# Gate and up weights side by side on two queues, and a new written order around the handover to the gate/up stage

## The chip, the core and the metric

The kernel runs on one core of one Trainium2 chip. A core has five engines that run their own instruction streams and meet through semaphores: TensorE (PE; its weight loads are listed as PEld), VectorE (DVE), ScalarE (ACT), GpSimd (POOL) and SyncE (SP). Transfers are started from SP or ACT and run on sixteen DMA engines. The metric is the time of one execution on the device, in microseconds (us); lower is better.

## What is computed

A pre-LayerNorm block on 2048 tokens of width 448 in bf16: a linear attention with 16 heads of 28, and a gated feed-forward of width 1792, each with a residual.

```python
def _A_ref(x, wqkv, wo):
    q, k, v = qkv[0], qkv[1], qkv[2]              # x @ wqkv, 16 heads of 28
    phi = lambda t: jnp.where(t > 0, t + 1, jnp.exp(t)) + 1e-6
    pq, pk = phi(q), phi(k)
    kv = jnp.einsum("bhsd,bhse->bhde", pk, v)     # sums over all tokens
    z = jnp.einsum("bhsd->bhd", pk)
    num = jnp.einsum("bhqd,bhde->bhqe", pq, kv)
    den = jnp.einsum("bhqd,bhd->bhq", pq, z)[..., None] + 1e-6
    o = num / den
    return o.reshape(B, S, D) @ wo
def _B_ref(x, w_gate, w_up, w_down):
    h = _gelu(x @ w_gate) * (x @ w_up)
    return h @ w_down
h = x + _A_ref(_layernorm(x), A_wqkv, A_wo)
h2 = h + _B_ref(_layernorm(h), B_w_gate, B_w_up, B_w_down)
```

The sum over all tokens parts the kernel in two: no token's attention output exists before the last token's k and v.

## The kernel before

The 2048 tokens are 16 tiles of 128. All work is cut into named tasks, each on one engine; a task waits by semaphores for the tasks whose data it reads or whose buffers it overwrites. In which order an engine runs its tasks is written out by hand in five strings, `ORDERS`, one for each of PE, ACT, DVE, POOL and SP; an engine goes through its string strictly in turn. The names, with the tile's number behind them:

- Start: `warm0`, `warm1` are matmuls of ones that only keep PE busy; POOL writes `ones`, `ident` and the zero columns of `o_sb` (`opad`, `opad2`). DVE takes the statistics (`bnst`, `bnag`), ACT `ln` and `rstd`, DVE or POOL the normalized tile (`norm`). Tiles 0 to 3 are transposed on PE (`tr`, evacuated by ACT's `ev`), tiles 4 to 15 by DMA transposes on SP (`xT`).
- k and v: `k`, `v` (PE), then phi(k): `ek` (ACT), `cl` (a clamp, POOL), `ph` (DVE), and `evv` (ACT) for v; `acc` adds to the kv sums in banks 6 and 7; DVE's `kz1`, `kz2` mask them.
- q: eight tasks for four chunks of 512 tokens, each in two halves, `qa` and `qb`; phi(q) by `eq`, `rq` (ACT), `cq`, `pq`.
- Attention output: `nd` (PE), `rd`, `om` (DVE: reciprocal, product), then o transposed. For tiles 0 and 1 PE does it (`tro`, evacuated by ACT's `evo`), for the others DMA transposes on SP (`oT`). `wo` (PE) and `hr` (DVE, the residual) follow; then the second LayerNorm (`hbnst`, `hbnag`, `hln` and `hrstd` on ACT, or `vpe`, `pow` on POOL; `normh`), `wrap` (DVE copies columns again behind the row) and the transposed tile: PE's `trh` with `evh` for tiles 0 and 1, SP's `hT` for the others.
- Gate and up: `gu0` to `gu55`, in chunks of 2, 2, 4, 4 and 4 tiles; ACT's `ge` (gelu, two per task) and DVE's `hm` (the product, two per task). Then `down`, `out` (DVE) and `dout` (SP).

Most matmuls use half of the array: a pair works on rows 0 to 63 and 64 to 127 at once. A product then comes in two tasks (k and v, qa and qb, `nd2a` and `nd2b`, `wo4a` and `wo4b`), the second with the row groups exchanged between two PSUM banks, and so it waits for the first. `tro`, `trh`, `wo0` and `wo1` use all 128 rows.

The gate and up weights lie in one tile `wgu_sb`, gate in partitions 0 to 63, up in 64 to 127. SP loads them in fourteen pieces, gate and up in turn, behind the last `xT` and the four `wo` loads and ahead of `oT2`, `oT3` and the load of the down weights (`dwd`). A gate/up task of the first two chunks computes two blocks of 128 columns for 256 tokens in 28 matmuls; a task of the later chunks one block for 512 tokens in 14.

Of the kernel before, what the change touches and what calls it, by code (L numbers as in the profile page):

```python
# [912 lines left out]
```

## Time and profile before

| | us |
|---|---|
| runs shown: median (lowest to highest of 3) | 196.68 (196.2 to 196.69) |
| the profiled execution | 196.7 |
| its span, first to last instruction | 194.9 |
| PE busy | 190.3 |
| DVE busy | 116.3 |
| ACT busy | 78.2 |
| POOL busy | 42.0 |
| granted TensorE clock, mean | 0.999 |

The span is what the trace covers; the rest of an execution's time lies around it. A row of the timeline begins with start and duration in us, then engine, line, operation, the tile written and those read, the shapes, how many instructions it stands for, and in brackets how long the engine was idle before it and what ended that. Rows overlap where instructions are pipelined, so that the distance of two starts tells more than a duration. In the chain of work the program is followed back from its last instruction; each row is a stretch with the engine and line that held it. All matmuls that come in pairs have one line, that of a helper (L430), and are told apart by their tiles.

### The profile page before, as it was taken

How to read it: one execution, taken by the hardware profiler on the slowest of the kernel's cores; microseconds unless marked ns; L12 is line 12 of the kernel's file. 1: busy time of each engine (PE TensorE's matmuls, PEld its weight loads, DVE VectorE, ACT ScalarE, POOL GpSimd, SP SyncE). 2: the span in 40 equal slices, each digit the busy share in tenths (PEclk: the TensorE clock that was granted, in tenths of full speed). 3: DMA queues.
4: the chain of work that ended last, by engine and by line, in shares of the span. 5: the costliest groups of instructions: out<-in, count | busy, mean ns of one | idle time of the engine just before them, and what ended most of it. 6: DMA issues, size and time to landing. Idle time of an engine off the chain costs nothing.

```text
span 194.9 us, 5336 instructions
## 1 busy us (share of the span) xinstructions
PE 190.3 (98%) x2192; PEld 137.9 (71%) x2192; DVE 116.3 (60%) x301; ACT 78.2 (40%) x205; POOL 42.0 (22%) x90
## 2 busy tenths in 40 slices
PE   7999999999999999999999999999999999999994
PEld 7556658754588977976675577877778779899554
DVE  2989735368998946843967745756735443431512
ACT  3689866669784212220442441233232442411100
POOL 3099974300050310500500500500500000000000
PEclk9999999999999999999999999999999999999999
DMA  6944558999836052152062250172040000010111
GB/s 191 377 116 97 81 110 185 247 248 205 260 103 110 15 101 50 50 105 62 10 129 46 46 106 2 30 117 51 5 94 28 23 0 0 3 47 3 47 47 47
DMA packets 37256, 17.53 MB, mean 90 GB/s; under 512 B 28272, under 2 KB 36336, under 8 KB 37232
## 3 DMA queue, kind: packets, MB, share of 16 engines
q1 hardware_dynamic: 36352, 16.45, 36.8%
q10 hardware_dynamic: 880, 0.75, 1.2%
q8 instruction: 17, 0.28, 0.6%
q14 instruction: 7, 0.06, 0.1%
HBM read 8.72 MB, written 1.84 MB: 54 GB/s over the span
## 4 chain that ended last, share of the span: by engine, by line
PE 96%; issue 1%; ACT 1%; DVE 1%; POOL 0%; DVEq 0%; ACTq 0%; POOLq 0%
PE ps L430 87%; PE ps L780 6%; PE ps L454 2%; DVE x_sb L660 1%; PE ps L495 1%; ACT xn L617 1%; PE ps L681 0%; ACT xnT L523 0%; PE ps L672 0%; DVE x_sb L756 0%; POOL ones_bf L395 0%; POOL eps_t L398 0%; ACT pqT L616 0%; DVEq L196 0%; ACTq L196 0%
## 5 line engine op out<-in xcount | busy, mean ns | idle before, releaser
L430 PE MATMUL ps<-hnT,wgu_sb 64*128 64x512 bf16 (+1 forms) x980 | 90.4, 333 | 0.0
L430 PEld LDWEIGHTS ps<-hnT,wgu_sb 64*128 64x128 bf16 x980 | 64.5, 94 | 18.6 <-DVE hh L832 1.7
L830 ACT ACTIVATE gl<-ps 128x256 bf16<-128x256 f32 x112 | 36.9, 381 | 89.3 <-PE ps L430 88.2
L832 DVE TENSOR_TENSOR hh<-ps,gl 128x256 bf16<-128x256 f32 x112 | 42.5, 415 | 35.7 <-ACT gl L830 31.5
L430 PE MATMUL ps<-wd_sb,hh 64*128 64x448 bf16 x336 | 34.4, 349 | 0.0
L430 PEld LDWEIGHTS ps<-wd_sb,hh 64*128 64x128 bf16 x336 | 25.6, 94 | 6.2 <-DVE x_sb L756 0.2
L430 PE MATMUL ps<-wkv_sb,xnT 64*128 64x448 bf16 x192 | 22.4, 350 | 0.4 <-ACT xnT L523 0.4
L462 DVE BATCH_NORM_STATS2 st<-x_sb 128x6 f32<-128x448 bf16 x32 | 18.7, 611 | 2.6 <-DMA x_sb<-in_A_x_dram 2.6
L756 DVE TENSOR_TENSOR x_sb<-ps,x_sb 128x448 bf16<-128x448 f32 (+1 forms) x17 | 9.9, 591 | 16.6 <-PE ps L430 9.8
L474 POOL TENSOR_SCALAR ln<-mv 128x2 f32<-128x2 f32 x7 | 1.6, 223 | 75.0 <-DVE mv L463 74.9
L568 DVE SCALAR_TENSOR_TENSOR pk<-ps,tm 128x448 bf16<-128x448 f32 x16 | 9.8, 620 | 9.6 <-POOL tm L566 7.1
L430 PE MATMUL ps<-xnT,wq_sb 64*128 64x512 bf16 x112 | 14.9, 377 | 0.2 <-ACT xn L617 0.2
L430 PEld LDWEIGHTS ps<-wkv_sb,xnT 64*128 64x128 bf16 x192 | 10.1, 94 | 6.3 <-issue 0.8
L430 PE MATMUL ps<-wo_sb,oT 64*128 64x448 bf16 x98 | 12.1, 350 | 0.1
L660 DVE TENSOR_TENSOR x_sb<-ps,x_sb 128x448 bf16<-128x448 f32 x16 | 9.4, 618 | 4.6 <-PE ps L430 4.4
L780 PE MATMUL ps<-wd_sb,hh 128*128 128x448 bf16 (+1 forms) x70 | 10.8, 315 | 0.0
L566 POOL TENSOR_SCALAR tm<-e 128x448 bf16<-128x448 bf16 x16 | 8.9, 559 | 6.4 <-ACT e L565 5.5
L487 POOL TENSOR_SCALAR hn<-x_sb,nm,rs 128x448 bf16<-128x448 bf16 x14 | 10.0, 720 | 0.8 <-POOL rs L476 0.2
L565 ACT ACTIVATE e<-ps 128x448 bf16<-128x448 f32 x16 | 8.5, 541 | 3.5 <-PE ps L430 2.2
L780 PEld LDWEIGHTS ps<-wd_sb,hh 128*128 128x128 bf16 x70 | 6.7, 98 | 4.3 <-issue 0.4
L655 DVE TENSOR_TENSOR o_sb<-ps,rd 128x448 bf16<-128x448 f32 x16 | 9.4, 612 | 0.1
L570 ACT ACTIVATE v<-ps 128x448 bf16<-128x448 f32 x16 | 8.4, 542 | 2.1 <-PE ps L430 2.1
(69 smaller groups left out, 140.4 us busy)
## 6 DMA issues: line engine op xcount, KB each, us to landing
out_dram<-x_sb SPq DMA_DIRECT2D x15, 112.0 KB, 1.7
wgu_sb<-in_B_w_gate_dram SPq DMA_DIRECT2D x7, 224.0 KB, 6.1
wgu_sb<-in_B_w_up_dram SPq DMA_DIRECT2D x7, 224.0 KB, 6.4
wd_sb<-in_B_w_down_dram SPq DMA_DIRECT2D x1, 1568.0 KB, 8.3
x_sb<-in_A_x_dram SPq DMA_DIRECT2D x2, 448.0 KB, 5.3
wkv_sb<-in_A_wqkv_dram ACTq DMA_DIRECT2D x2, 336.0 KB, 3.7
x_sb<-in_A_x_dram SPq DMA_DIRECT2D x3, 224.0 KB, 4.2
wo_sb<-in_A_wo_dram SPq DMA_DIRECT2D x2, 336.0 KB, 4.4
```

Of the source, the lines that this page charges most:

```text
L430: ins = e.matmul(o_, l_, r_, start=s_, stop=p_, **kw)
L462: op("dve", lambda e: e.bn_stats(st[:, t, :], src_ap), [b_src], [b_st[t]], "%sbnst%d" % ("" if mv is mv1 else "h", t), 0.53, key, after=after)
L487: return lambda e: e.tensor_scalar(dst, src[:, t, :], nm[:, t:t + 1], rs[:, t:t + 1], ALU.add, ALU.mult)
L565: act_exp(lambda e: e.activation(e1[:, ie, :], oK, AF.Exp), bank(bk), [b_e1[ie]], "ek%d" % t, _c_act(D), kk)
L566: op("pool", lambda e: e.tensor_scalar(tm1[:, ie, :], e1[:, ie, :], 1.0 + EPS, 0.0, ALU.min, ALU.max), [b_e1[ie]], [b_tm1[ie]], "cl%d" % t ...
L568: op("dve", lambda e: e.scalar_tensor_tensor(pk[:, i, :, 0:GW], psK3, EPS, tm1[:, ie, :].rearrange("p (g e) -> p g e", g=NG), ALU.max, ALU ...
L655: op("dve", lambda e: e.tensor_tensor(o_sb[:, so, oc:oc + D].rearrange("p (a e) -> p a e", e=28), nd3[:, :, 0:28], rd[:, i, :].unsqueeze(2 ...
L660: op("dve", lambda e: e.tensor_tensor(h_sb[:, u, :], ps[:, b, 0:D], x_sb[:, u, :], ALU.add), bank(b) + [b_x[u]], [b_h[u]], "hr%d" % u, 0.5 ...
L756: op("dve", lambda e: e.tensor_tensor(x_sb[:, t, c0:c1], ps[:, bk, c0:c1], h_sb[:, t, c0:c1], ALU.add), bank(bk) + [b_h[t]], [bo], "out%d% ...
L780: ins = e.matmul(ps[:, bk, c0:c1], hh[:, j, hsl(t)], wd_sb[:, j, c0:c1], start=(j == 0), stop=(j == NJ - 1))
L830: G.add("act", lambda e, gi=gi, cs_=cs_, psG=psG: e.activation(gl[:, gi, cs_], psG[:, cs_], AF.Gelu_apprx_tanh), r=bank(BK_G[i]), w=[b_glh ...
L832: op("dve", lambda e, dst=dst, srcU=srcU, srcL=srcL: e.tensor_tensor(dst, srcU, srcL, ALU.mult), bank(BK_U[i]) + [b_glh], [b_ar[j_][t % HR ...
```

## The change

Gate and up weights: the fourteen pieces on SP become two transfers, `dwg` on SP in the old place and `dwu` on ACT, which first waits for the last `xT`. The two transposing tasks `tro0` and `tro1` of four 128-row transposes each become one task of sixteen transposes of 64 rows, in pairs, into banks 6 and 7; it waits for `om0` and `om1`, and `evo0` and `evo1` each read both banks. The gate/up tasks of two column blocks become two tasks of 14 matmuls, `a` and `b`; `ge` and `hm` stay as they were. The clamps of tiles 14 and 15 move from POOL to DVE. `trh` waits for its `wrap` only ahead of its seventh transpose. `warm0` has 33 matmuls where it had 38. All five orders are written anew.

```diff
-    WARM = 38
+    WARM = 33
+    CL_DVE = cfg.get("cl_dve", (14, 15))
...
-        for k in range(7):
-            prev = [dma(wgu_sb[0:64, k, :], wg3[:, k, :], [b_wg[k]], "dwg%d" % k, 64 * FF * 2, after=prev, key=20.0)]
-            prev = [dma(wgu_sb[64:128, k, :], wu3[:, k, :], [b_wu[k]], "dwu%d" % k, 64 * FF * 2, after=prev, key=20.0)]
+        prev = [dma(wgu_sb[0:64, :, :], wg3, [*b_wg], "dwg", 7 * 64 * FF * 2, after=prev, key=20.0)]
+        dma(wgu_sb[64:128, :, :], wu3, [*b_wu], "dwu", 7 * 64 * FF * 2, q="act", r=[b_xnT[T - 1]], key=20.0)
...
-            op("pool", lambda e: e.tensor_scalar(tm1[:, ie, :], e1[:, ie, :], 1.0 + EPS, 0.0, ALU.min, ALU.max),
+            op("dve" if t in CL_DVE else "pool", lambda e: e.tensor_scalar(tm1[:, ie, :], e1[:, ie, :], 1.0 + EPS, 0.0, ALU.min, ALU.max),
...
             def ftro(e):
                 ins = None
-                for k in range(4):
-                    ins = e.transpose(tvo[:, k, :], o_sb[:, so, k * 128:(k + 1) * 128], ident[:])
+                for t in (0, 1):
+                    for k in range(4):
+                        for b, rows in ((P, A_), (Q, B_)):
+                            ins = e.transpose(psb[:, b, (4 * t + k) * 64:(4 * t + k + 1) * 64], o_sb[rows, t % O_R, k * 128:(k + 1) * 128], ident[rows, rows])
...
-            G.add("pe", ftrh, r=[b_hn[sh], b_hnd[sh], b_ident], w=bank(bh), name="trh%d" % t, dur=_c_mm(128, 7), key=ka)
+            G.add("pe", ftrh, r=[b_hn[sh], (b_hnd[sh], 6), b_ident], w=bank(bh), name="trh%d" % t, dur=_c_mm(128, 7), key=ka, mw=True, pdt=_c_mm(128))
...
-                a, b = [], []
                 for jj in range(nj):
                     j = j0 + jj
+                    a, b = [], []
...
-                pe_pairs("gu%d" % v, both(a, b), N, [b_hnT[t % HR] for t in tiles] + [(x, 2 * k) for k, x in enumerate(b_wg)] + [(x, 2 * k + 1) for k, x in enumerate(b_wu)],
+                    pe_pairs("gu%d%s" % (v, "ab"[jj] if nj > 1 else ""), both(a, b), N,
```

Of the orders, these three places matter for the prediction. First PE at the handover from attention to gate/up, before, from `tro1` on. `xnT,wq_sb` are the halves of the q tasks (8 matmuls `qa`, 6 `qb`), `ident,o_sb` is `tro`, L688 with L689 `wo1` and then `wo0`, `wo_sb,oT` with 8 and 6 `wo2a` and `wo2b`, `ident,hn` both `trh`, `kvz,pqT` `nd4a` and `nd4b`, behind which `gu1` begins.

```order
L681 MATMUL ps<-ident,o_sb 128x128 x4
L430 MATMUL ps<-xnT,wq_sb 128x512 x6
L688 MATMUL ps<-wo_sb,oT 128x448 x3
L689 MATMUL ps<-wo_sb,oT 128x448
L688 MATMUL ps<-wo_sb,oT 128x448 x3
L689 MATMUL ps<-wo_sb,oT 128x448
L430 MATMUL ps<-xnT,wq_sb 128x512 x8
L430 MATMUL ps<-wo_sb,oT 128x448 x8
L430 MATMUL ps<-xnT,wq_sb 128x512 x6
L430 MATMUL ps<-wo_sb,oT 128x448 x6
L702 MATMUL ps<-ident,hn 128x128 x14
L430 MATMUL ps<-kvz,pqT 128x116 x16
```

The same place after (L703 with L704 is `wo0`, then `wo1`; L687 the joined `tro`); behind the last row come `nd4a`, `gu1a`, `nd4b` and `gu1b`.

```order
L687 MATMUL ps<-ident,o_sb 128x64 x16
L432 MATMUL ps<-xnT,wq_sb 128x512 x14
L703 MATMUL ps<-wo_sb,oT 128x448 x3
L704 MATMUL ps<-wo_sb,oT 128x448
L432 MATMUL ps<-xnT,wq_sb 128x512 x6
L703 MATMUL ps<-wo_sb,oT 128x448 x3
L704 MATMUL ps<-wo_sb,oT 128x448
L432 MATMUL ps<-wo_sb,oT 128x448 x8
L432 MATMUL ps<-xnT,wq_sb 128x512 x8
L432 MATMUL ps<-wo_sb,oT 128x448 x6
L719 MATMUL ps<-ident,hn 128x128 x14
L432 MATMUL ps<-xnT,wq_sb 128x512 x6
```

`wo0` moved ahead of `qb21` (the first six q matmuls), `wo2a` ahead of `qa31` (eight), `qb31` behind both `trh`; `nd4a` and `nd4b` are parted by the first half of `gu1`, `nd2a` and `nd2b` stand together. In the same way `wo4a` and `wo4b`, which followed each other, have `gu4a` between them.

Second ACT at the same place, before. L616 (L618 after) is `eq`, L617 (L619) `rq`, L684 (L693) `evo`.

```order
L616 ACTIVATE pqT<-ps 112x2x512
L684 ACTIVATE oT<-ps 128x512
L616 ACTIVATE pqT<-ps 112x2x512
L617 ACTIVATE xn<-ps 112x1024 x2
L467 ACTIVATE ln<-mv,eps_t 128x1
```

And after:

```order
L693 ACTIVATE oT<-ps 128x512 x2
L619 ACTIVATE xn<-ps 112x1024
L618 ACTIVATE pqT<-ps 112x2x512
L619 ACTIVATE xn<-ps 112x1024
L618 ACTIVATE pqT<-ps 112x2x512
L469 ACTIVATE ln<-mv,eps_t 128x1
```

Before, the rows are `eq12`, `evo1`, `eq10`, then `rq10` and `rq12`; after, `evo1` and `evo0`, then `rq12`, `eq12`, `rq10`, `eq10`: `rq12` now runs ahead of the pair of q task 2,1 (`rq10` and `eq10`).

Third ACT about 6 us earlier, where the up load now stands, after (L567 is `ek13`, then `ek14`; L572 `evv13`); SP keeps the gate load alone between the `wo` loads and `oT2`.

```order
L567 ACTIVATE e<-ps 128x448
L366 DMA wgu_sb<-in_B_w_up_dram 64x7x1792
L572 ACTIVATE v<-ps 128x4x112
L567 ACTIVATE e<-ps 128x448
L572 ACTIVATE v<-ps 128x4x112
```

Before, no transfer stands among ACT's instructions behind the start. On SP the fourteen issues became one. On POOL `norm13` stood ahead of `norm12` and now stands behind `norm15`, `norm14` and `cl8`; `ones` stood first and now stands behind `eps`, `mhalf`, `opad` and `mones`.

More of the change, by code (lines that the diff above doesn't have):

```diff
@@ L14 @@
 ORDERS = (
[43 rows of a table removed]
[39 rows of a table added]
+    "eps mhalf opad mones ones powwarm mask_a opad2 ident mask_b mask_c negm4 cl0 norm4 norm5 negm6 cl1 norm6 norm7"
[4 rows of a table added]
     "dx0 dx1 dx2 dwv_t dx4 dx6 dx8 dx12 dwq dwq_t dwq_u pqones xT4 xT5 xT6 xT7 xT8 xT9 xT10 xT11 xT12 xT13 xT14 xT15"
[3 rows of a table removed]
[3 rows of a table added]
 )
@@ L565, in kv_tile @@
             act_exp(lambda e: e.activation(e1[:, ie, :], oK, AF.Exp), bank(bk), [b_e1[ie]], "ek%d" % t, _c_act(D), kk)
-            op("pool", lambda e: e.tensor_scalar(tm1[:, ie, :], e1[:, ie, :], 1.0 + EPS, 0.0, ALU.min, ALU.max),
-               [b_e1[ie]], [b_tm1[ie]], "cl%d" % t, 0.53, kk)
+            op("dve" if t in CL_DVE else "pool", lambda e: e.tensor_scalar(tm1[:, ie, :], e1[:, ie, :], 1.0 + EPS, 0.0, ALU.min, ALU.max),
+               [b_e1[ie]], [b_tm1[ie]], "cl%d" % t, _c_dve(D, 4.0) if t in CL_DVE else 0.53, kk)
             op("dve", lambda e: e.scalar_tensor_tensor(pk[:, i, :, 0:GW], psK3, EPS, tm1[:, ie, :].rearrange("p (g e) -> p g e", g=NG), ALU.max, ALU.add),
@@ L661, in res_h, with nd_first @@
             ln_stats(u, h_sb[:, u, :], b_h[u], st2, mv2, b_st2, b_mv2, ka)
-        def a2_first(t):
+        def nd_first(t):
             ka = -20.0 + 0.1 * t
-            bnd, bh = FIRST_BK[t]
-            so = t % O_R
+            bnd = FIRST_BK[t][0]
             def fnnd(e):
@@ L675, in a2_first, with tro_first @@
             nd_evac(t, bnd, 0, ka)
-            tvo = psb[:, bh, 0:512].rearrange("p (k t) -> p k t", k=4)
+        def tro_first():
+            P, Q = FIRST_BK[0][1], FIRST_BK[1][1]
             def ftro(e):
                 ins = None
-                for k in range(4):
-                    ins = e.transpose(tvo[:, k, :], o_sb[:, so, k * 128:(k + 1) * 128], ident[:])
-                return ins
-            G.add("pe", ftro, r=[b_o[so], b_ident], w=bank(bh), name="tro%d" % t, dur=_c_mm(128, 4), key=ka)
-            op("act", lambda e: e.activation(oT[:, so, :, :], tvo, AF.Identity), bank(bh), [b_oT[so]], "evo%d" % t, _c_act(512), ka)
+                for t in (0, 1):
+                    for k in range(4):
+                        for b, rows in ((P, A_), (Q, B_)):
+                            ins = e.transpose(psb[:, b, (4 * t + k) * 64:(4 * t + k + 1) * 64], o_sb[rows, t % O_R, k * 128:(k + 1) * 128], ident[rows, rows])
+                return ins
+            G.add("pe", ftro, r=[b_o[0], b_o[1], b_ident], w=bank(P, Q), name="tro0", dur=0.054 * 8, key=-19.9, mode=64, rg={P: "A", Q: "B"})
+            for t in (0, 1):
+                tvo = psb[:, P:Q + 1, t * 256:(t + 1) * 256].rearrange("p b (k t) -> p k b t", t=64)
+                ov_ = oT[:, t % O_R, :, :].rearrange("p k (b t) -> p k b t", t=64)
+                op("act", lambda e, tvo=tvo, ov_=ov_: e.activation(ov_, tvo, AF.Identity), bank(P, Q), [b_oT[t % O_R]], "evo%d" % t, _c_act(512), -19.8)
+        def a2_first(t):
+            ka = -20.0 + 0.1 * t
+            bnd, bh = FIRST_BK[t]
+            so = t % O_R
             def fnwo(e):
@@ L696, in a2_first, with ftrh @@
             tvh = psb[:, bh, 0:896].rearrange("p (k t) -> p k t", k=7)
-            def ftrh(e):
+            def ftrh(e, W):
                 ins = None
-                for k in (0, 1, 2, 4, 5, 6, 3):
+                for n, k in enumerate((0, 1, 2, 4, 5, 6, 3)):
+                    if n in (0, 6):
+                        W(n)
                     ko = k * 128 if k < 4 else (k - 4) * 128 + 64
@@ L810, in gu_chunk @@
                         b.append(mm(psU[:, jj * N:(jj + 1) * N], wgu_sb[B_, k, j * 128:(j + 1) * 128], hnT[B_, kb_, c0:c0 + N], k == 0, k == 6))
-                pe_pairs("gu%d" % v, both(a, b), N, [b_hnT[t % HR] for t in tiles] + [(x, 2 * k) for k, x in enumerate(b_wg)] + [(x, 2 * k + 1) for k, x in enumerate(b_wu)],
-                         [(b_ps[BK_G[i]], 0), (b_ps[BK_U[i]], 1)], kb, {BK_G[i]: "A", BK_U[i]: "B"})
+                    pe_pairs("gu%d%s" % (v, "ab"[jj] if nj > 1 else ""), both(a, b), N,
+                             [b_hnT[t % HR] for t in tiles] + [(x, 2 * k) for k, x in enumerate(b_wg)] + [(x, 2 * k + 1) for k, x in enumerate(b_wu)],
+                             [(b_ps[BK_G[i]], 0), (b_ps[BK_U[i]], 1)], kb + 0.01 * jj, {BK_G[i]: "A", BK_U[i]: "B"})
                 WH = W_ // 2
@@ L837, in gu_chunk @@
             vcount[0] = v
+        for t in (0, 1):
+            nd_first(t)
+        tro_first()
         done = 0
```

92 rows, old and new, of the table ORDERS are left out of this document.

## The prediction

> **What bounds the kernel now.** I read the page's first part, then the chain in order of time, then the timeline around the two places where that chain leaves TensorE, then the transfers.
>
> ```profile
> span 194.9 us, 5336 instructions
> PE 190.3 (98%) x2192; PEld 137.9 (71%) x2192; DVE 116.3 (60%) x301; ACT 78.2 (40%) x205; POOL 42.0 (22%) x90
> ```
>
> ```profile
> 43.85 0.33 PE ps L681 x4
> ...
> 49.08 0.14 issue
> 49.21 3.02 PE ps L430 x28
> ...
> 52.26 1.17 DVE x_sb L660 x2
> ...
> 62.84 40.46 PE ps L430 x552
> ...
> 103.35 78.37 PE ps L430 x776
> ```
>
> TensorE is busy 190.3 of 194.9 us, and from 62.84 us to its last 11 us the chain is nothing but its matmuls. The change removes no matmul of the gate, up, down, q, k or v products. So only three things can be won: idle time of TensorE (mostly at 47 to 54 us, the handover from attention to the gate/up stage, where the chain comes from ACT at 49.08 and passes to DVE at 52.26), the small stops between its tasks, and the start. Anything above about 3 us either way would need a transfer that arrives late.
>
> **The handover, task by task.** Times are us from the span's start; "x8" and "x6" with `wq_sb` are the two halves of a q task.
>
> ```profile
> 43.48 0.38 PE L430 MATMUL ps<-kvz,pqT 64*128 64x116 bf16 x8
> ...
> 44.33 1.68 PE L430 MATMUL ps<-xnT,wq_sb 64*128 64x512 bf16 x14
> ...
> 46.27 0.82 PE L430 MATMUL ps<-xnT,wq_sb 64*128 64x512 bf16 x6
> ...
> 46.37 0.60 ACT L684 ACTIVATE oT<-ps 128x512 bf16<-128x512 bf16 x1 [0.17 <-PE ps L681]
> ...
> 47.02 0.74 PE L688 MATMUL ps<-wo_sb,oT 128*128 128x448 bf16 x3
> ...
> 47.13 1.02 ACT L616 ACTIVATE pqT<-ps 112x1024 bf16<-112x1024 f32 x1 [0.16 <-PE ps L430]
> ...
> 47.99 0.74 PE L688 MATMUL ps<-wo_sb,oT 128*128 128x448 bf16 x3
> ...
> 48.05 1.93 ACT L617 ACTIVATE xn<-ps 112x1024 bf16<-112x1024 f32 x2
> ...
> 49.21 1.04 PE L430 MATMUL ps<-xnT,wq_sb 64*128 64x512 bf16 x8 [0.19 <-ACT xn L617]
> ...
> 52.16 0.95 PE L702 MATMUL ps<-ident,hn 128*128 128x128 bf16 x14
> ...
> 53.33 0.61 DVE L709 COPY hnT<-ps 128x896 bf16<-128x896 bf16 x1
> ...
> 53.47 0.82 PE L430 MATMUL ps<-kvz,pqT 49*128 49x116 bf16 x15 [0.21 <-DVE x_sb L660]
> ...
> 53.91 0.38 PE L430 MATMUL ps<-kvz,pqT 64*128 64x116 bf16 x8
> ...
> 54.13 2.13 PE L430 MATMUL ps<-hnT,wgu_sb 64*128 64x256 bf16 x36
> ```
>
> Before, qa31 (49.21) waits for ACT to empty the banks of q task 2,1 (eq10 at 47.13, rq10 from 48.05), while wo1 and wo0 fill that wait; then trh (52.16) is followed by a wait for the two residual adds on DVE, until nd4a at 53.47; nd4a and nd4b directly behind each other take 53.91 - 53.47 = 0.44 for what is 0.22 when another task stands between (54.13 - 53.91): a stop of 0.22.
>
> The new order I step through from nd2a at 43.5, the work ahead of it being the same. The two removed transposes (tro0 and tro1) took 0.33 each by the chain. Their successor is sixteen 64-row transposes, which I price from this row of twenty:
>
> ```profile
> 9.76 0.75 PE L495 MATMUL ps<-ident,xn 64*128 64x64 bf16 x20
> ```
>
> That is 16/20 x 0.75 = 0.60, against 0.66. nd2a and nd2b now adjoin (0.44 + 0.22), so tro ends at 44.75. qb30 and qa21 take 45.94 - 44.33 = 1.61 (45.94 is where the second tro stood, 0.33 ahead of 46.27), to 46.35. evo1 and evo0, 0.6 each (46.37), end about 46.0, in time. wo0 takes 47.99 - 47.02 = 0.97, to 47.3; qb21 takes 47.02 - 46.27 = 0.75, to 48.05. Now ACT: rq10 can start only behind qb21, at 48.15, and eq10 0.92 later (48.05 - 47.13), ending at 50.1; rq12 and eq12, now ahead of them, fit into 46.0 to 47.9 at two times 0.92 and so cost nothing. qa31 starts at 50.1 + 0.14 = 50.2, that is 1.0 later than before. But wo1 (0.97) and wo2a (0.76, a share of the 3.02) stand ahead of it, to 49.8, so only 0.4 is idle. Then qa31 0.86, wo2b 0.6, trh 0.9 and qb31 0.7 run to 53.3. The residual adds of tiles 2 and 3 (1.17 by the chain) start at 51.85 and end under trh and qb31; evh1 (0.61) ends at 53.6, and gate/up begins about 53.7 with 0.22 of nd4b still owed: 53.9 against 54.13. I take **-0.3**, bounded by +0.3 (two waits of ACT or DVE 0.3 later than I have them) and by -0.9 (0.43 idle ahead of 53.47, 0.22 of nd4, 0.24 of the wait at 49.21, all saved).
>
> **Adjoining halves in the gate/up stage.** Halves whose row groups swap stop TensorE when nothing stands between them. wo4a and wo4b adjoined before, wo6a stood apart:
>
> ```profile
> 61.77 1.81 PE L430 MATMUL ps<-wo_sb,oT 64*128 64x448 bf16 x14
> ...
> 63.42 1.69 PE L430 MATMUL ps<-hnT,wgu_sb 64*128 64x256 bf16 x28
> ```
>
> ```profile
> 72.60 0.93 PE L430 MATMUL ps<-wo_sb,oT 64*128 64x448 bf16 x8
> ...
> 73.35 1.71 PE L430 MATMUL ps<-hnT,wgu_sb 64*128 64x256 bf16 x28
> ```
>
> 14 matmuls took 1.65 there; 8 took 0.75 apart, so 14 need 1.31. The split gate/up task gu4a goes between: **-0.33**. The splitting itself adds no instruction and no wait: both parts write the same two banks with the same row groups, ACT and DVE still wait for the second part. acc13b/acc13a newly adjoin, acc15b/acc15a no longer do: 0. Later orders (from wo10 on) move halves between the same kinds of neighbours: 0, between -0.1 and +0.4, since no row shows a price for them.
>
> **The start.**
>
> ```profile
> 0.99 0.31 POOL L403 MEMSET o_sb<- 128x256 bf16 x1
> ...
> 1.93 4.24 PE L454 MATMUL ps<-ones_bf 128*128 128x128 bf16 x38
> ```
>
> Five warming matmuls fewer save 5 x 4.24/38 = 0.55. But ones_bf, for which they wait, now stands behind eps, mhalf, the memset of o_sb (0.31) and mones: 0.4 later. **-0.15**, between -0.3 and +0.3 (norm0, on DVE, then ends the wait instead).
>
> **Edits that I cost at nothing.** The columns behind the stretch are busy times of PE, PEld, DVE, ACT and POOL.
>
> ```profile
> 30.00:40.00 10.00, 9.94 (x138) 7.41 (x135) 4.56 (x8) 5.65 (x12) 3.98 (x7) 1.00 0.90 234
> ```
>
> Clamping tiles 14 and 15 on DVE shortens their path to kz1, which TensorE does not wait for: qa11 (40.4 to 41.4) covers it. The late wait of trh saves one wrap copy only where trh waits for it, and by the walk above hn is ready. The up transfer's issue on ACT takes one issue (0.60 on SP, below) between ek13 and evv13, where ACT has room (5.65 busy of 10 here); if that cover were gone, 0.6 would fall on the path. norm13 moves behind norm15, norm14 and cl8 on POOL, so xT13, and behind it on SP xT14, xT15, the wo loads and the gate load, are issued about 2.5 later; k13 to k15 come late enough.
>
> **The transfers.**
>
> In the first two rows the last three columns are granted clock, DMA share and GB/s.
>
> ```profile
> 38.00:40.00 2.00, 2.00 (x28) 1.00 1.05 247
> ...
> 52.00:54.00 2.00, 1.73 (x30) 1.00 1.09 372
> ```
>
> ```profile
> 11.65 16.94 SPq L526 DMA_TRANSPOSE xnT<-xn  x12
> 28.64 3.19 SPq L364 DMA_DIRECT2D wo_sb<-in_A_wo_dram  x4
> ...
> 40.91 0.60 SPq L364 DMA_DIRECT2D wgu_sb<-in_B_w_up_dram  x1
> 45.48 2.51 SPq L729 DMA_TRANSPOSE oT<-o_sb  x2
> 48.03 0.58 SPq L364 DMA_DIRECT2D wd_sb<-in_B_w_down_dram  x1
> ```
>
> ```profile
> wgu_sb<-in_B_w_up_dram SPq DMA_DIRECT2D x7, 224.0 KB, 6.4
> ...
> oT<-o_sb SPq DMA_TRANSPOSE x14, 2.5
> ```
>
> The fourteen weight pieces, each into 64 partitions, move at 247 GB/s with the DMA engines full (share 1.05); the down weights, into all 128, at 372. The last piece, issued at 40.91, lands about 47.3. Gate/up needs them at 54, so their speed does not count by itself. It counts through oT2 and oT3, queued behind the gate load on SP's queue: wo2a needs them at 49.0 in the new order (it came at 50.07 before). The gate load is now issued near 34.3 (28.64 + 3.19 + 2.5), the up load near 35. From about 35.2 on, the 14 x 224 KB = 3.2 MB take 13.0 at 247 GB/s, to 48.2, or 8.6 at 372, to 43.8. Both halves are written at once, as in the 372 row, so I take the nearer end, 372: then oT3, issued at 46.4, lands at 48.9. **0**, and +1.25 at the other end (rival 1).
>
> [...] No row shows two halves in flight on two queues.
>
> **Sum.** -0.3 - 0.33 - 0.15 = -0.78, and +0.1 for the third gate/up task:
>
> ```profile
> 56.35 0.75 DVE L832 TENSOR_TENSOR hh<-ps,gl 128x256 bf16<-128x256 f32 x2
> ```
>
> Its banks were freed at 57.10, 0.1 before TensorE came for them (54.13 + 2 x 1.53); TensorE now comes 0.2 earlier and the ACT table load no earlier. -0.68 on the profiled execution's 196.7 (its span 194.9 and 1.8 around it), which stands level with the median of 196.68: **196.0 us**.
>
> **Rivals.**
> 1. *Late weights* (slower). If the two queues together stay at 247 GB/s, oT2 and oT3 wait behind the gate load until 48.2 and oT3 lands near 50.7 (2.51 for the two). wo2a then ends at 51.45 rather than 49.8; qa31, which would have started at 50.2, starts 1.25 later: -0.68 + 1.25 = +0.57, 197.3. Each microsecond by which the weights end later still (a gate load held up more by xT13) adds one. It decides from the point where oT3 lands after 50.1. For it: share 1.05 at 247 GB/s. Against: 372 GB/s into 128 partitions. Chance 0.2.
> 2. *The gain is lost on DVE* (no change). DVE is 60% busy over the span and nearly full between 56 and 72; hm7 and hm11 now stand behind two pq products and two residual outputs. Two stops of 0.3 at gu9 or gu13 give 196.6. For it: the margin of 0.1 above. Chance 0.15.
> 3. *ACT holds the handover up* (slower). If the up load blocks ACT until xT15 has landed, or rq12/eq12 slip past qb21, eq10 ends up to 1.5 later and qa31 with it: 197.2. Chance 0.1.
> 4. *More is won* (the bound of -0.9 in the handover, no third-task stop, -0.3 at the start): -1.5, 195.2. Chance 0.08.
>
> **Chances and range.** My own case holds 0.47, at 195.5 to 196.6. By 0.3% (0.59 us: about what a measurement of this kernel can tell from no change) the bounds lie at 196.09 and 197.27. My case falls two thirds below the first: 0.32 faster, 0.15 same. Rival 1: 0.06 same, 0.14 slower; rival 2: 0.02 faster, 0.13 same; rival 3: 0.02 same, 0.08 slower; rival 4: 0.08 faster. Together 0.42 faster, 0.36 same, 0.22 slower; as the 0.4 for later orders is a bound with nothing under it, I shift 0.06 from same to slower: 0.42, 0.30, 0.28. The range 195.2 to 197.6 leaves out the far ends of rivals 1, 3 and 4.
>
> **What would show it.** Right: in the chain, qa31 near 50.2 and the first gate/up matmul near 53.7; no 1.8-us group of 14 wo matmuls for tiles 4 and 5; 300 GB/s or more at 36 to 44; oT3 landed before 49.5. Wrong: TensorE waiting for a transfer at wo2a; waits of PE for DVE hh after 56; a DMA issue on ACT well over 0.6; or the clock granted to TensorE rising later because fewer matmuls warm it.

## The result, and the profile after

| | before | after |
|---|---|---|
| median of 6 runs each, us | 196.48 (196.16 to 196.69) | 201.0 (200.56 to 203.11) |
| ratio | 1 | 1.0253 (95% interval 1.0206 to 1.03) |
| profiled execution, span | 196.7, 194.9 | 200.83, 199.1 |
| granted clock, mean over the span | 0.999 | 0.991 |

The change costs 4.5 us; 201.0 lies well above the range of 195.2 to 197.6. Of the kernels further down, a run over 1.5% above the fastest of its kernel is left out of the ratio, but not of the median. The first part of the page after:

```profile
span 199.1 us, 5327 instructions
PE 190.8 (96%) x2195; PEld 128.2 (64%) x2195; DVE 117.7 (59%) x303; ACT 78.4 (39%) x205; POOL 41.4 (21%) x88
```

PE is busy 0.5 us longer in a span that is 4.2 us longer, so most of the loss shows as idle time. The chain of work shows where:

```profile
44.27 0.24 PE ps L687 x16
...
46.53 5.21 DMA oT<-o_sb
51.74 0.14 issue
51.87 3.77 PE ps L432 x21
```

From 46.53 to 51.74 the end waits for a DMA transpose: oT3, which `wo2a` needs. The timeline of PE at the same place; the name in the first bracket is that of a releaser long done, the real one is oT2, just as oT3 is in the second:

```profile
47.56 0.74 PE L703 MATMUL ps<-wo_sb,oT 128*128 128x448 bf16 x3
48.24 0.36 PE L704 MATMUL ps<-wo_sb,oT 64*128 64x448 bf16 x1
51.35 0.35 PE L432 MATMUL ps<-wo_sb,oT 64*128 64x448 bf16 x1 [2.75 <-DVE hn L710]
51.87 0.94 PE L432 MATMUL ps<-wo_sb,oT 64*128 64x448 bf16 x7 [0.18 <-DMA oT<-o_sb]
52.46 2.07 PE L432 MATMUL ps<-xnT,wq_sb 64*128 64x512 bf16 x8
53.99 1.66 PE L432 MATMUL ps<-wo_sb,oT 64*128 64x448 bf16 x6
```

PE came to `wo2a` at 48.6 (48.24 + 0.36) and stood for 2.75 and 0.18 us. Then `qa31`, 1.04 us long before, took 2.07, and `wo2b` 1.66 (0.90 in e1, below, where the clock stayed full). The table by stretches says why (columns: PE busy and matmuls, granted clock, DMA share, GB/s):

```profile
38.00:40.00 2.00, 1.93 (x28) 1.00 1.01 192
...
42.00:44.00 2.00, 1.94 (x26) 1.00 1.03 388
44.00:46.00 2.00, 2.00 (x39) 1.00 1.05 321
46.00:48.00 2.00, 2.00 (x15) 1.00 1.03 204
...
50.00:52.00 2.00, 0.47 (x3) 1.00 0.94 245
52.00:54.00 2.00, 2.00 (x16) 0.66 1.09 380
54.00:56.00 2.00, 2.00 (x14) 0.50 0.76 261
```

Behind the idle stretch the clock is granted at half for 3.41 us (52.63 to 56.04), under `wo2a`, `qa31`, `wo2b` and `trh`. The last column tells the other half of the story: 388 GB/s for two to four microseconds, but 192 and 204 on both sides of them, where one of the two loads is in flight alone. The transfers on SP's queue, and the two loads from issue to landing:

```profile
12.05 20.09 SPq L528 DMA_TRANSPOSE xnT<-xn  x12
32.18 2.40 SPq L366 DMA_DIRECT2D wo_sb<-in_A_wo_dram  x4
34.62 0.67 SPq L366 DMA_DIRECT2D wgu_sb<-in_B_w_gate_dram  x1
45.26 2.54 SPq L746 DMA_TRANSPOSE oT<-o_sb  x2
```

```profile
wgu_sb<-in_B_w_up_dram ACTq DMA_DIRECT2D x1, 1568.0 KB, 13.9
wgu_sb<-in_B_w_gate_dram SPq DMA_DIRECT2D x1, 1568.0 KB, 16.1
```

The `xT` end 3.5 us later than before (32.18 against 28.64); the gate load, issued at 34.62, lands at 50.7 and the two transposes right behind it. The gate/up stage then begins at 57.54 where it began at 54.13: 3.4 of the 4.2 us. Between 88 and 119 us (`ge12` to `ge27`) the first activation of each gate task, matched by name, stands 3.64 to 3.69 us behind before, and the last 11 us begin 4.16 us later (185.88 against 181.72).

### The profile page after: what moved, and what is told of

It reads as the page before. It is cut to its first block, busy times and chain, and to the rows that moved or that the text cites. A ratio compares the mean times of both kernels' runs of the same rounds, so it can differ in the third digit from the quotient of the medians.

```text
span 199.1 us, 5327 instructions
## 1 busy us (share of the span) xinstructions
PE 190.8 (96%) x2195; PEld 128.2 (64%) x2195; DVE 117.7 (59%) x303; ACT 78.4 (39%) x205; POOL 41.4 (21%) x88
## 4 chain that ended last, share of the span: by engine, by line
PE 88%; DMA 5%; DVE 2%; ACT 2%; issue 1%; SPq 0%; DVEq 0%
PE ps L432 81%; PE ps L797 5%; DMA x_sb<-in_A_x_dram 3%; DMA oT<-o_sb 3%; DVE st L464 1%; DVE hh L850 1%; ACT L871 1%; PE ps L719 1%; ACT gl L848 1%; ACT pqT L618 1%; SPq L366 0%; PE ps L497 0%; PE ps L673 0%; PE ps L703 0%; DVE x_sb L773 0%
## 5 line engine op out<-in xcount | busy, mean ns | idle before, releaser
L432 PE MATMUL ps<-hnT,wgu_sb 64*128 64x512 bf16 (+1 forms) x980 | 92.0, 333 | 0.2
L432 PEld LDWEIGHTS ps<-hnT,wgu_sb 64*128 64x128 bf16 x980 | 58.4, 94 | 27.2 <-DVE hh L850 4.7
L432 PE MATMUL ps<-wd_sb,hh 64*128 64x448 bf16 x336 | 35.3, 349 | 0.0
L432 PEld LDWEIGHTS ps<-wd_sb,hh 64*128 64x128 bf16 x336 | 25.1, 94 | 6.7
L432 PE MATMUL ps<-wo_sb,oT 64*128 64x448 bf16 x98 | 14.0, 363 | 3.0 <-DVE hn L710 2.8
L432 PE MATMUL ps<-xnT,wq_sb 64*128 64x512 bf16 x112 | 15.7, 394 | 0.0
L432 PEld LDWEIGHTS ps<-wkv_sb,xnT 64*128 64x128 bf16 x192 | 8.8, 94 | 7.0 <-issue 0.5
L432 PEld LDWEIGHTS ps<-wo_sb,oT 64*128 64x128 bf16 x98 | 7.7, 97 | 5.9 <-DVE hn L488 3.0
L483 POOL TENSOR_SCALAR nm<-mv 128x2 f32<-128x2 f32 x13 | 3.3, 253 | 36.2 <-DVE mv L465 35.8
L567 ACT ACTIVATE e<-ps 128x448 bf16<-128x448 f32 x16 | 8.7, 541 | 2.5 <-PE ps L432 2.1
```

The source lines that it names most:

```text
L432: ins = e.matmul(o_, l_, r_, start=s_, stop=p_, **kw)
L483: op("pool", lambda e: e.tensor_scalar(nm[:, a:b], mv[:, a:b, 0], -1.0, None, ALU.mult), b_mv[a:b], b_nm[a:b], "%snegm%d" % ("" if mv is m ...
L567: act_exp(lambda e: e.activation(e1[:, ie, :], oK, AF.Exp), bank(bk), [b_e1[ie]], "ek%d" % t, _c_act(D), kk)
```

## The experiments

In the kernel after the clock stood at half for one stretch of 3.41 us, which makes its mean 0.991 (0.5 x 3.41 / 199 = 0.009). Such a stretch is called a half-clock window here; where an execution without a profile has 0.991, one is taken from this sum, and two where it has 0.983. Medians are over all runs listed with a result; "gate/up" is the start of the first gate/up matmul and "oT3" the moment at which its landing let the rest of `wo2a` start, both in the profiled execution.

| kernel | median, us | ratio to before (95%) | oT3 | gate/up | half clock at |
|---|---|---|---|---|---|
| before | 196.4 to 196.6 | | no wait | 54.13 | none |
| after | 201.0 | 1.0253 (1.0206 to 1.03) | 51.87 | 57.54 | 52.6 |
| e1 pieces on SP | 200.27 | 1.016 (1.0112 to 1.0209) | 51.20 | 55.37 | none |
| e2 norm13 early | 201.09 | 1.0211 (1.0175 to 1.0247) | 53.54 | 57.71 | 7.4 |
| e3 before, norm13 late | 199.71 | 1.0158 (1.0109 to 1.0206) | 52.02 | 57.74 | 52.2 |
| e4 qa31 first | 199.04 | 1.0119 (1.0101 to 1.0137) | 52.70 | 56.24 | none |
| e5 norm13 early, pieces | 197.26 | 1.0048 (1.0022 to 1.0073) | 49.98 | 54.15 | none |
| e6 and 38 warm-ups | 197.54 | 1.0046 (1.0029 to 1.0063) | 49.87 | 54.03 | none |
| e7 before, two queues | 199.78 | 1.0143 (1.0093 to 1.0193) | 52.24 | 57.92 | 52.2 |
| e8 before, 33 warm-ups | 196.37 | 1.0 (0.9984 to 1.0016) | no wait | 53.77 | none |
| e9 = e5, late orders of before | 196.85 | 1.0033 (1.0008 to 1.0058) | 49.22 | 53.39 | none |
| e10 = e9, oT ahead of last pieces | 196.63 | 1.0028 (1.0001 to 1.0055) | 49.42 | 53.59 | none |
| e12 before, whole loads on SP | 199.49 | 1.0134 (1.0076 to 1.0192) | 52.30 | 57.94 | 52.2 |
| e13 = e9, 38 warm-ups | 197.27 | 1.0046 (1.003 to 1.0063) | 49.61 | 53.78 | none |
| e14 after, 38 warm-ups | 201.61 | 1.0256 (1.0217 to 1.0294) | 52.12 | 57.97 | 52.5 |
| e15 = e13, transposes earlier | 197.46 | 1.004 (1.0028 to 1.0052) | 50.04 | 54.21 | none |
| e16 after, wait filled | 200.46 | 1.0223 (1.0174 to 1.0271) | 52.70 | 56.88 | none |

### First theory: the late norm13 alone

**e1.** The load of each weight in seven pieces again, alternating on SP.

```diff
-        prev = [dma(wgu_sb[0:64, :, :], wg3, [*b_wg], "dwg", 7 * 64 * FF * 2, after=prev, key=20.0)]
-        dma(wgu_sb[64:128, :, :], wu3, [*b_wu], "dwu", 7 * 64 * FF * 2, q="act", r=[b_xnT[T - 1]], key=20.0)
+        for k in range(7):
+            prev = [dma(wgu_sb[0:64, k, :], wg3[:, k, :], [b_wg[k]], "dwg%d" % k, 64 * FF * 2, after=prev, key=20.0)]
+            prev = [dma(wgu_sb[64:128, k, :], wu3[:, k, :], [b_wu[k]], "dwu%d" % k, 64 * FF * 2, after=prev, key=20.0)]
```

> The kernel after with one thing undone: the gate and up weights again as 14 alternating pieces on SP's queue, nothing on ACT's queue; all else (norm13 last on POOL, qa31 behind wo2a) as after. Theory A (the transposes of x end 3.5 us later, since norm13 is last on POOL, and all behind them on SP is late; the two queues are not the cause): 14 pieces at 247 GB/s take 13 us from about 36.5 us on, so oT2 and oT3 land at 51 to 52 us again, TensorE waits at wo2a, the clock is halved for a window: 200.5 to 201.5 us. Theory B (the two queues are the cause, each at half rate while alone): the time falls to 198 us or less.

Measured 200.27 (198.51 to 201.8): near theory A, B alone falls. PE still waited, until 50.66 and 51.20:

```profile
50.66 0.35 PE L434 MATMUL ps<-wo_sb,oT 64*128 64x448 bf16 x1 [2.42 <-DVE hn L713]
51.20 0.91 PE L434 MATMUL ps<-wo_sb,oT 64*128 64x448 bf16 x7 [0.19 <-DMA oT<-o_sb]
```

This execution had the full clock throughout and took 198.51; the one with mean clock 0.983 took 201.8.

**e2.** The other part undone, on POOL (and on ACT the matching copies `dup13`, `dup14`, `dup15` in that order):

```diff
- norm12 cl6 cq3 cq2 cl7 norm15 norm14 cl8 norm13 cl9
+ norm12 norm13 cl6 cq3 cq2 cl7 norm14 norm15 cl8 cl9
```

> The kernel after with POOL's order of the norms of tiles 13, 14, 15 as before (norm13 right behind norm12, then norm14, norm15) and ACT's dup13, dup14, dup15 in that order; the two queues and all else as after. Theory A: the transposes of x end at about 28.7 us in place of 32.1, the gate load is issued at about 31.3, both loads overlap for most of their way and have landed by 45.5 us, oT2 and oT3 by 48.5 us; TensorE does not wait at wo2a and the clock stays full: 196.0 to 196.8 us. Theory B (two queues): a wait at wo2a of over 1 us stays, 198 us or more. Theory C (the order wo2a ahead of qa31, or the parted gate/up tasks, cost the time): unchanged near 200.8 us.

Measured 201.09: theory A, as the only cause, is wrong. The `xT` take 16.67 us again as before, the gate load is issued at 33.50, and still oT3 lets `wo2a` go on only at 53.54. (About 1.5 us of that is the start of this execution: the clock was halved from 7.4 to 10.9 us, see e8, and the first `xT` is issued at 13.51 in place of 12.05.) What I had assumed, that both loads overlap and then move at nearly 390 GB/s, did not happen: 206 to 229 GB/s in every stretch of 2 us from 36 to 48 us.

**e3.** The late norm13 put into the kernel before:

```diff
- norm13 norm12 cl6 negm14 cq3 cq2 cl7 norm14 opad2 norm15 cl8 powwarm
+ norm12 cl6 negm14 cq3 cq2 cl7 norm15 norm14 opad2 cl8 norm13 powwarm
```

> The kernel before with one thing of the change: norm15, norm14, norm13 in that order on POOL with norm13 behind cl8, and ACT's dup15, dup14, dup13 behind ek8; weights on one queue, all else as before. Theory A: the transposes of x end near 32 us, the weights start about 3.4 us later, oT2 and oT3 land at about 52.5 us in place of 48.9 and 49.4; qa31 stands ahead of wo2a here and covers a part, so TensorE waits 1.5 to 2.5 us at wo2a: 198 to 200.5 us. Theories B and C: no change, 196.5 us.

Measured 199.71, as theory A has it: 198.45 and 199.13 with the full clock, 200.3 and 200.63 with one half-clock window.

```profile
11.35 20.64 SPq L528 DMA_TRANSPOSE xnT<-xn  x12
32.03 2.40 SPq L366 DMA_DIRECT2D wo_sb<-in_A_wo_dram  x4
```

So the late norm13 is enough for a loss of 2 to 4 us, with pieces on one queue and the order of before. It is a cause; e2 says that there is a second.

**e4.** In PE's order of the kernel after, `wo2a qa31` became `qa31 wo2a`.

> The kernel after with one place of TensorE's order undone: qa31 ahead of wo2a, as before; all else as after. Theory A: oT2 and oT3 still land at 51.3 and 51.7 us; qa31 runs inside the wait (8 matmuls, about 1 us), so the longest idle of TensorE falls below 2 us, and the clock should stay full: 1 us from qa31 and up to 1.7 us from the clock are won, 198.2 to 199.0 us; if the clock is halved all the same, 199.8 us. Theory C (the order of these two alone is the cause): 197 us or less.

Measured 199.04, all four runs within 0.9 us of each other and all with the full clock. Theory A's figure came out, though not by its two terms: oT3 landed later still in this execution, and `qa31` won nothing by itself.

```profile
49.69 1.04 PE L433 MATMUL ps<-xnT,wq_sb 64*128 64x512 bf16 x8 [1.16 <-ACT pqT L619]
52.17 0.35 PE L433 MATMUL ps<-wo_sb,oT 64*128 64x448 bf16 x1 [1.44 <-DVE hn L711]
52.70 1.72 PE L433 MATMUL ps<-wo_sb,oT 64*128 64x448 bf16 x13 [0.18 <-DMA oT<-o_sb]
```

The wait is as long but parted, and no half clock follows. The order of the two tasks is not the cause of the wait; it decides whether the wait is one stretch. That it alone keeps the clock full is not shown: e3 above and e7 and e12 below have `qa31` first too, and half of their runs have a half-clock window.

### Second theory: two causes of late weights

Theory D: the late norm13 and the whole loads each make the weights late enough to stop `wo2a`.

**e7.** The two loads alone, in the kernel before: the opposite of the diff of e1, with `dwu` behind `ek13` on ACT.

> The kernel before with one thing of the change: gate weights as one load on SP, up weights as one load on ACT's queue, issued behind ek13. Theory D: the loads follow each other at about 205 GB/s, about 16 us from 33.5 us on, so the last lands at 49.5 to 51 us, and oT2 and oT3 with it or right behind it, in place of 48.9 and 49.4; qa31 covers a part: 198 to 200.5 us. Against D (two queues side by side at 390 GB/s, as the 42 to 44 us stretch of the kernel after showed): weights landed by 43 us, oT2 and oT3 at 48 us, 196.0 to 196.6 us.

Measured 199.78 (198.35 and 199.11 with the full clock, 200.46 and 201.35 with one window): theory D. In its table by stretches and its list of transfers

```profile
36.00:38.00 2.00, 1.94 (x37) 1.00 1.00 199
38.00:40.00 2.00, 1.97 (x29) 1.00 1.04 206
...
44.00:46.00 2.00, 2.00 (x26) 1.00 1.02 201
46.00:48.00 2.00, 2.00 (x14) 1.00 1.04 204
```

```profile
wgu_sb<-in_B_w_gate_dram SPq DMA_DIRECT2D x1, 1568.0 KB, 15.2
wgu_sb<-in_B_w_up_dram ACTq DMA_DIRECT2D x1, 1568.0 KB, 17.0
```

the DMA engines are full at about 205 GB/s, where the fourteen pieces in the kernel before had 240 to 259:

```profile
40.00:42.00 2.00, 1.93 (x32) 1.00 1.07 259
42.00:44.00 2.00, 2.00 (x27) 1.00 1.03 242
```

Counting in the trace the 3584-byte descriptors begun in a microsecond, by queue:

```
                       e7, two queues                      after
at us          SP queue   ACT queue   median ns   SP queue   ACT queue   median ns
37                56           0         290          0          68         287
39                57           0         294          3          56         273
41                21          45       218-247       38          43       180-184
43                 3          52         292         57          53         145
45                 3          54         292         59          10       242-249
47                 0          58         293         53           0         293
```

In e7 the load on ACT's queue hardly moves until that on SP's queue is nearly done. A descriptor took 290 to 294 ns in e7 while nearly all of them wrote the same 64 partitions (37, 39, 43 to 47 us), and 145 ns in the kernel after at 43 us, where 57 of one load's began beside 53 of the other's. (In the first and the last microsecond of a load alone it was near 140 too: in the kernel after 140 at 36 us and 140 to 146 at 49 and 50 us, and in e7 at 34 and at 50 us, when 2 to 13 of the load's descriptors were in flight in place of 16.) The gate load had landed at 31.93 + 15.2 = 47.1, yet oT2 and oT3, on the same queue, came out behind the up load of the other queue (oT2 at 51.6, oT3 at 52.1): being on another queue put nothing out of their way. In which order a single DMA engine serves the two loads is not shown: the trace does not tell the engines apart, and the counts are those of all sixteen.

**e12.** The kernel before with the same two whole loads, but both on SP:

```diff
-        dma(wgu_sb[64:128, :, :], wu3, [*b_wu], "dwu", 7 * 64 * FF * 2, q="act", r=[b_xnT[T - 1]], key=20.0)
+        prev = [dma(wgu_sb[64:128, :, :], wu3, [*b_wu], "dwu", 7 * 64 * FF * 2, after=prev, key=20.0)]
```

> The kernel before with the gate weights as one load and the up weights as one load, both on SP's queue, one behind the other; nothing on ACT's queue. If each DMA engine serves a whole load of 64 partitions through before the next (so that at any time nearly all write the same 64 partitions, 290 ns per 3584-byte descriptor, 205 GB/s), it does not matter on how many queues they are: up landed at 49.5 to 50.5 us, oT3 at 51.5 to 52.5, and 198.3 to 199.2 us with full clock, 200.3 to 201.4 with a half-clock window, as e7_before_two_queues. If the second queue was the harm (its descriptors waiting for the first queue), one queue is as before: 196.6 us.

Measured 199.49 (198.34 and 198.47 with the full clock, 200.51 and 201.43 with less), like e7:

```profile
38.00:40.00 2.00, 2.00 (x30) 1.00 1.06 210
...
46.00:48.00 2.00, 2.00 (x14) 1.00 1.02 201
```

The harm is not in the second queue but in the whole loads, each into 64 partitions: 199.78 with two queues (e7), 199.49 with one.

**e5.** Both undone at once: the edits of e1 and e2 in the kernel after.

> The kernel after with two things undone together: the norms of tiles 13 to 15 in the order of before, and the gate and up weights as 14 pieces on SP. Theory D (two causes of late weights, each enough alone: the transposes of x end 3.5 us later, and the two whole loads are served one after the other by each DMA engine at about 205 GB/s, 16 us in place of 13): with both undone oT2 and oT3 land by 49 us and TensorE does not wait at wo2a. Theory E (the start: 33 warm-up matmuls end before the first rows of x are there, and a window of half clock follows in some executions, 1.5 us): a run has 195.8 to 196.6 us where the clock stays full at the start and 197.3 to 198.1 us where not. If neither D nor E holds, the time stays over 198.5 us in all runs.

Measured 197.26 (196.84 to 198.07): 3.7 us of the 4.4 are back, D holds; what it had wrong is that TensorE would not wait at all, for 0.65 and 0.17 us are left. The transposes and the handover:

```profile
11.80 16.79 SPq L530 DMA_TRANSPOSE xnT<-xn  x12
```

```profile
49.46 0.35 PE L434 MATMUL ps<-wo_sb,oT 64*128 64x448 bf16 x1 [0.65 <-issue]
49.98 0.91 PE L434 MATMUL ps<-wo_sb,oT 64*128 64x448 bf16 x7 [0.17 <-DMA oT<-o_sb]
```

Gate/up begins at 54.15, as before. What the new order wins ahead of `wo2a` is spent there.

### The clock

**e16.** Into the kernel after, between `wo1` and `wo2a`, goes a task that reads nothing of the block and whose result is overwritten:

```diff
+            def fill(e):
+                ins = None
+                for _ in range(44):
+                    ins = e.matmul(ps[:, bh, 0:128], ones_bf[:], ones_bf[:], start=True, stop=True)
+                return ins
+            if t == 0:
+                G.add("pe", fill, r=[b_ones], w=bank(bh), name="fill", dur=2.4, key=ka)
```

> The kernel after with one task more on TensorE: 44 matmuls of ones (128 x 128, into bank 6, which is free there) between wo1 and wo2a, so that it is not idle while it waits for oT2. Weights, transposes and orders are those of the kernel after, so oT2 and oT3 land at 51.3 and 51.7 us as before. If the half-clock window at 52.6 to 56.0 us comes from the idle stretch, it goes: 199.0 to 199.5 us, runs without a 0.991 mean clock (but for the start). If the clock falls for another reason: 200.8 us, unchanged.

```profile
48.35 2.63 PE L712 MATMUL ps<-ones_bf 128*128 128x128 bf16 x44
52.16 0.36 PE L433 MATMUL ps<-wo_sb,oT 64*128 64x448 bf16 x1 [1.18 <-DMA oT<-o_sb]
...
53.28 1.21 PE L433 MATMUL ps<-xnT,wq_sb 64*128 64x512 bf16 x8
```

`wo2a` started 0.8 us later than in the kernel after (52.16, 51.35), gate/up 0.66 earlier (56.88, 57.54), with a clock of 1.00 from 46 to 60 us: the way between the two took 1.5 us less than under the half clock, which did not come in this execution, where 1.18 us of the idle stretch were left in place of 2.75. In the time this is 200.46 against 201.0 only: three of the four runs had the full clock (199.86 to 200.65), one 0.991 (202.66), and in the profiled one 0.6 us was lost again between 68 and 78 us (the activations stand 2.9 us behind before until 68 us, 3.4 from 78 us). The expected time was missed on the high side.

**e8, e14, e6, e13.** Theory E asks whether the shorter warm-up leaves TensorE at half clock for one window of the start in some executions. For the start: 33 warm-up matmuls ahead of `warm1` in the kernel before (e8); `warm1` first, 38 and `ones` first on POOL in the kernel after (e14), in e5 (e6) and in e9 (e13). The edit of e8:

```diff
-    WARM = 38
+    WARM = 33
```

> The kernel before with one thing of the change: warm0 ahead of warm1 and 33 warm-up matmuls in place of 38. Theory E: the warm-up ends 0.5 us earlier, TensorE then stands idle until x is normalised, and in some executions, not in all, a window of 3.41 us is granted half clock between 7 and 11 us: runs of 196.0 to 196.7 us and runs of 197.6 to 198.4 us beside each other. Without E: all within 0.3 us of 196.5 us.

> The kernel after with the start of before alone: warm1 ahead of warm0, 38 warm-up matmuls, ones first on POOL; two queues and late norm13 stay. Theory E: the spread upward (203.1 and 202.0 us beside 200.6 to 201.2) goes, while the wait at wo2a stays: 199.0 us where the clock stays full, 200.5 to 201.0 us where a half-clock window follows the wait, nothing over 201.3 us. Without E: runs of 202 us and more remain.

> As e5_norm13_and_pieces, and the start of before too: warm1 ahead of warm0, 38 warm-up matmuls in place of 33, ones first on POOL. Left of the change are the joined transposes of o, the parted gate/up tasks with wo4a, gu4a, wo4b, clamps 14 and 15 on VectorE and the orders. Theory E: all runs within 0.5 us of each other, 195.6 to 196.4 us. Without E: the same spread as e5_norm13_and_pieces.

> As e9_late_orders, and the start of before: warm1 ahead of warm0, 38 warm-up matmuls, ones first on POOL. Runs of e9_late_orders stand in two groups, 196.3 to 197.0 us and 197.5 to 198.2 us. Theory E (the shorter and later warm-up sometimes leaves TensorE at half clock for one window more at the start): only the lower group is left, 195.9 to 196.6 us, and the median is under that of before, about 196.2 us. Without E: the two groups stay.

e8: nine of ten runs at 196.28 to 196.70, one at 197.74; the second group that E expects is one run of ten, and the median does not differ. e14: 201.61 (199.76 to 202.53), three of six runs with a mean clock of 0.983, so theory E does not explain the spread of the kernel after. Where a second half-clock window lies, which 0.983 makes likely, no profiled execution shows. e6: 197.13 to 197.62 and one 200.35 with 0.991, where E had 195.6 to 196.4. e13: one group, 196.95 to 197.75, but not the lower of the two of e9 (E had 195.9 to 196.6). E's times failed in these three. What can be shown is that the start can go wrong with 33: in e2's profile

```profile
6.00:8.00 2.00, 1.38 (x24) 0.86 1.09 371
8.00:10.00 2.00, 1.94 (x13) 0.50 1.09 380
```

the clock falls to half behind an idle 1.07 us between warm-up and first transpose. How often, and whether the upper groups of e9 and e10 (below) are that, stays open: no execution of those groups was profiled.

### What is left

**e9, e10.** e5 with the orders of before from `gu29`, `ge29`, `hr13` and `hT12` on (e9), and then oT2 and oT3 ahead of the last two pieces, without their tie to the last piece (e10):

```diff
- dwg6 dwu6 oT2 oT3 dwd
+ oT2 oT3 dwg6 dwu6 dwd
```

> As e5_norm13_and_pieces, and the order of all engines from the last quarter on (TensorE from gu29 on behind wo12b, ScalarE from ge29, VectorE from hr13, hbnst13, SP from hT12) as before. In e5_norm13_and_pieces the gate activations stand 0.15 us behind those of before until 112 us, and the end 0.6 us. If the late orders cost that: 196.8 us, 0.45 us under e5_norm13_and_pieces. If not: 197.26 us, unchanged.

> As e9_late_orders, and the transposes oT2 and oT3 on SP ahead of the last two weight pieces (k = 6 of gate and up), which are then issued behind them. In e5_norm13_and_pieces oT3 landed at 49.84 us and TensorE stood 0.65 and 0.17 us at wo2a. If the weights ahead of oT2 and oT3 in the DMA engines are what hides the gain of the handover, oT3 lands by 48.7 us, that wait goes, and the last pieces land by 52 us, before gu1a at 54 us needs them: 0.6 to 0.8 us under e9_late_orders, 196.1 us. If not: no change against e9_late_orders, or a new wait of up to 1 us at gu1a for the last piece.

e9: 196.85, the expected figure, in two groups (196.27 to 197.04 and 197.45 to 198.22) and one run of 199.38. That it came out is luck in part, for the profiled execution shows a second reason beside the late orders: oT3 landed earlier, 2.6 us from its issue, `wo2a` went on at 49.22 (0.76 ahead of e5), and gate/up began 0.74 us ahead of before. The bracket names DVE, but what the second row waits for is oT3.

```profile
48.71 0.35 PE L434 MATMUL ps<-wo_sb,oT 64*128 64x448 bf16 x1
49.22 0.91 PE L434 MATMUL ps<-wo_sb,oT 64*128 64x448 bf16 x7 [0.17 <-DVE x_sb L665]
...
53.39 0.94 PE L434 MATMUL ps<-hnT,wgu_sb 64*128 64x256 bf16 x14
```

Its gate activations stand 0.6 us ahead of before from 65 to 130 us and 0.44 at 169 us. In e5 they go from 0.15 behind to 0.6 at the end. So the last quarter costs 0.45 with the late orders of after, 0.2 of which is lost with those of before too. e10: 196.63, no different from e9, in the same two groups; oT3 let `wo2a` go on no earlier (49.42). The pieces ahead of it were not what set it there but its own way: oT2 now took 2.4 us from issue to landing where it took 3.4 in e9, but oT3, behind it on SP,

```profile
45.55 2.51 SPq L749 DMA_TRANSPOSE oT<-o_sb  x2
```

was issued only at 46.81 and took 2.5, as the transposes of o do in the median. In this order TensorE reaches `wo2a` at 48.9 (48.6 in after), before oT3 is there.

**e15.** e13 with two moves, against a stop at `wo8a` behind oT9:

```diff
- om8 hm11_1 hm11_0 om9
+ om8 om9 hm11_1 hm11_0
- hT5 dout0 oT8 oT9
+ hT5 oT8 oT9 dout0
```

> As e13_late_orders_warm38, with om9 right behind om8 on VectorE, and oT8, oT9 ahead of dout0 on SP. In e13_late_orders_warm38 oT9 landed at 87.45 us and TensorE stood 0.4 us at wo8a, where e9_late_orders did not; its gate activations go from 0.2 us ahead of before to 0.2 us behind there. If that stop is what is left between e13_late_orders_warm38 and e9_late_orders: 0.4 us under e13_late_orders_warm38, in one group, 196.5 to 197.0 us, the median at 196.8. A gain over before would need 196.1 us or less; not expected, since the last quarter loses another 0.2 us and the start stands where that of before does.

Measured 197.46: missed, the stop moved (its activations fall from 0.2 to 0.6 us behind before between 75 and 85 us). No kernel here is faster than before.

## Why the prediction was wrong

**The step that failed is "The transfers", priced at 0.** Of 247 and 372 GB/s I took "the nearer end, 372", since both halves would be written at once. They were not: the gate load stood behind the `xT` and `wo` loads, the up load did not, and they shared the engines for about four microseconds. From 36.5, when the first of their descriptors ran (I had 35.2), to 50.7 us the 3.2 MB moved at 226 GB/s, less than the pieces on one queue; e7 shows 199 to 225 from 36 to 48 us even when both are issued within 2.1 us. My range ended at the 247 of before, which a change could fall below.

**The edit at nothing that was not nothing: norm13.** I had seen the delay (2.5; it measured 3.5) and asked only whether k13 to k15 come late enough. The delay went on through SP to the gate load and to oT2 and oT3, where the cover was gone. I had walked it to 48.9 with the rate of 372; at 205 to 247 both together put oT3 at 51.7. Each alone costs 1.7 to 2.5 us with the full clock (e3, e7), both 2.4 in the median of e4: they fill the same wait, so their prices do not add.

**Rival 1 was the mechanism.** Its place, its sign and the sign by which it would show ("TensorE waiting for a transfer at wo2a") were right, its price was not. Two errors in it pulled apart: the last load landed 2.6 us later than the 48.2 it had, and oT3 came 1.0 behind that load instead of 2.5. By its own rule of one per microsecond, oT3 at 51.7 in place of 50.7 makes 198.3; the half clock, which it did not have, adds about 1.5 to 1.7 (e16; e3's pairs of runs), and the last quarter 0.45: 200.3 to 200.5, and with 0.17 more in the stops of gate/up (below) up to 200.6, against 200.83 measured. The rest is open. I gave this chain 0.2 and cut the range at 197.6, though nothing bounded it there.

**The handover, -0.3.** Right in sign, and larger than priced, where it could show: with oT3 letting `wo2a` go on at 49.22 gate/up begins at 53.39 (e9), 0.53 ahead of before with the 0.21 of `nd4b` still owed. The joined transposes took 0.24 by the chain and not the 0.60 that I had priced from the twenty of the start. In the kernel after all of it is spent in the wait.

**Adjoining halves, -0.33.** Right, and given back. After:

```profile
58.51 7.42 PE L432 MATMUL ps<-hnT,wgu_sb 64*128 64x256 bf16 x126
65.66 1.02 PE L432 MATMUL ps<-wo_sb,oT 64*128 64x448 bf16 x8
66.42 1.03 PE L432 MATMUL ps<-hnT,wgu_sb 64*128 64x256 bf16 x14
67.18 0.83 PE L432 MATMUL ps<-wo_sb,oT 64*128 64x448 bf16 x6
67.75 1.79 PE L432 MATMUL ps<-hnT,wgu_sb 64*128 64x256 bf16 x28
```

wo4a and wo4b take 0.76 + 0.57 = 1.33 in place of 1.65. But the 126 gate/up matmuls ahead of them take 65.66 - 58.51 = 7.15, 1.59 for 28, against 1.53 before: 0.27 is lost in stops for the product of an earlier task, where I had 0.1.

**The start, -0.15.** No gain: PE's unbroken stream begins at 10.60, before at 10.5. **Later orders**, 0 with bounds to 0.4: about 0.25 (the 0.45 of the last quarter less the 0.2 that e9 loses too). **Rivals 2 and 3** did not decide: the issue on ACT took 0.66, and the stops for DVE cost tenths.

## What to carry to other kernels

A task that is "late but covered" is covered only for its own readers: follow the queue it stands in to the last transfer behind it, and ask who waits for that one. Two whole loads on two queues were not two loads side by side here for more than about four microseconds; small alternating pieces moved at 240 to 293 GB/s (before, e1), whole loads at 199 to 225 on one queue or two (e12, e7). And price a wait of TensorE at its length plus what half a clock may cost the work behind it: behind the waits of e3 (1.45 us in all) and of the kernel after (2.93), 1.5 to 1.7 us in some executions, and in other executions of e3 nothing.
